# Attention and routed expert MLPs on one Trainium2 core: the overflow loop moved ahead of the last block's output, eight buffers of gathered rows, no weight conversion in a chunk with an output

## The chip, the core and the metric

The kernel runs on one core of one Trainium2 chip. The core has a matrix engine (PE, whose weight loads are listed apart as PEld), a vector engine (DVE), an activation engine (ACT), a general engine (POOL) that here also starts the gathers and scatters of rows, and a queue (SP) that starts the plain transfers. Each engine works through its own list of instructions in the order in which the program wrote them; engines wait for each other by semaphores. The metric is the device time of one execution in microseconds (us). Lower is better.

## The reference

The first half is attention inside chunks of 64 tokens, for 8 batches, 8 heads, 576 tokens and a head width of 64. Its output, seen as 4608 rows of 512 numbers, is `x`. The second half sends each row through one of eight experts, but only if its skip score is positive:

```python
skip_score = x @ w_skip
do_compute = skip_score > 0
out = x.copy()
xc = x[do_compute]
logits = xc @ w_gate
e_idx = np.argmax(logits, axis=1)
probs = softmax(logits)
gate_w = probs[np.arange(len(xc)), e_idx]
for e in range(E):
    mask = e_idx == e
    h = np.maximum(xc[mask] @ w1[e], 0.0)      # 512 -> 1024
    y[mask] = gate_w[mask, None] * (h @ w2[e]) # 1024 -> 512
out[do_compute] = xc + y
```

So the number of rows of each expert is known only while the kernel runs.

## The kernel before

The program has one launch and, in time, two stages.

**Stage 1, attention and routing (about the first 150 us).** 36 tiles of 128 tokens run through a software pipeline (lines 733 to 790): scores, exponent, transposes, products, then the logits and the routing, which gives each row a place in the list of its expert. The rows `x` are written to the output tensor as they come.

**Stage 2, the experts.** The experts are sorted by their number of rows, and each rank has a fixed capacity, cut into blocks of at most 128 rows (`BLOCKS`, line 50): 464, 400, 288, 288, 280, 248, 232 and 112 rows. 22 blocks form nine units: rank 0 is split in two (256 and 208 rows), and each other rank is one. In the text, unit 2 is the one with 400 rows, units 3 and 4 have 288, unit 5 has 280, unit 6 has 248, unit 7 has 232 and unit 8 has 112. Unit 0 and the first products of stage 2 overlap the end of stage 1. Rows beyond the capacities would be done by the overflow loop at the end (`For_i`, line 975), which runs a number of times that is computed on the chip (`nend`) and may be zero. Where it is zero, each engine still has to load the number, branch past the body and pass the loop's closing waits; these instructions carry the lines 974 and 975 in the profile.

To keep float32 accuracy in 16-bit products, every number is held as a high and a low half, and each product is three: high by high, high by low, low by high. One unit runs so:

1. *First layer*, `l1_steps` (line 512). The hidden width of 1024 is cut into `FC` = 8 chunks. For each chunk twelve matmuls are issued: eight with the high half of the chunk's weights, then four with the low half. `l1_out` follows with one ACT instruction (relu, line 527) and one DVE instruction (the low half, line 528). Three PSUM buffers `hp` take turns.
2. *Second layer*, `l2_steps` (line 540): 24 matmuls of 512 columns for a block of 128 rows, in four steps of six.
3. *Output of a block*, `blk_out` (line 555): one DVE instruction per part (line 561) that adds the gathered row, and then a scatter of the rows (POOL, line 221). Blocks of at most 32 rows have four parts, blocks of at most 64 have two. `blk_out` is a generator kept in the list `prev`, and `out_prev` advances it by one part; so a block's output is issued later, between the products of the next block or, for the last block of a unit, between the chunks of the next unit's first layer.

**Weights.** The weights arrive as float32, one chunk of both layers at a time (512 KB, `load_chunk`, line 206, four staging buffers, started by SP), and are turned into high and low halves by `conv_chunk` (line 212): an ACT instruction (line 217) for the high half and a DVE instruction (line 218) for the low half. There are 56 of these in stage 2, ranks 1 to 7 by 8 chunks, and three sets of converted weights.

What sets the place of a conversion in the order is a pacing clock written out by hand (lines 881 to 897). Each chunk and each step of six matmuls adds an amount of nanoseconds to `clock` by calling `spent`; whenever it reaches `PACE` = 2800, 2800 is taken off and one conversion, the next in the fixed order, is issued at that place of ACT's and DVE's lists. Before the matmuls of a chunk are issued, `need` issues at once whatever conversions up to that chunk haven't been issued yet.

```python
for m, done in enumerate(l1):
    if done:
        out_prev()
        spent(5 * n)
```

Here `done` is true once per chunk, and `n` is the number of rows of the unit. In the second layer each step adds 1280, and a step that also prepares the next unit's rows (`blk_xt`: transposes on PE, line 502, then ACT line 503 and DVE line 506) adds 1280 to the clock without issuing a conversion. The program keeps this order: the list is built under a manual schedule.

**Rows.** The rows of a block are fetched by `blk_gather` (line 491, an indirect transfer issued by POOL, line 221) into one of `XGB` = 6 buffers `xg`, which are cleared at the start (line 202). After block b has been issued, gathers up to block b + `XGB` - 1 are (line 966).

Of the kernel before, what the change touches and what calls it, by code (L numbers as in the profile page):

```python
# [32 lines left out]
FIRST = 3  # L33
EARLY = (3, 3, 4)
FIRST_UNIT = 2
XGB = 6
WSETS = 3
PACE = 2800.0
W_AT = (12, 14, 16, 18, 20, 22, 24, 26)
# [64 lines left out]
def moe_attention_kernel(ctx: ExitStack, tc: tile.TileContext, qk: bass.AP, vo: bass.AP, cst: bass.AP, crow: bass.AP, wall: bass.AP, out: bass.AP):  # L104
# [95 lines left out]

    for _ in range(XGB):
        nc.gpsimd.memset(spool.tile([P, DM], F32, name="xg", bufs=XGB), 0.0)

# [16 lines left out]
    def rows_dma(key, **kw):  # L220
        ins = nc.gpsimd.indirect_dma_start(**kw)  # L221
        ins = getattr(ins, "ins", ins)
        tc.declare_no_dep(ins, group=key, reason="row sets of different transfers are disjoint")
        tc.add_to_no_dep_group(key, ins)
# [33 lines left out]
    def bank(k=None):  # L258
        if k is None:
            turn[0] ^= 1  # L260
            k = turn[0]
        return ps_s.tile([P, DM], F32, name=f"sp{k}")
# [228 lines left out]
    def blk_gather(rec, n=P, rows=NTOK):  # L491
        xg = spool.tile([P, DM], F32, name="xg", bufs=XGB)
        rows_dma("out", out=xg[:n], out_offset=None, in_=out[:rows, :], in_offset=bass.IndirectOffsetOnAxis(ap=rec[0][:n], axis=0), bounds_check=rows - 1, oob_is_err=False)
        return xg
# [17 lines left out]
    def l1_steps(xt, w, ht, n, alloc, need):  # L512
        for fc in range(FC):
            need(fc)
            hp = alloc()[:, :n]
            m = 0
            for a, b in ((0, 0), (0, 1), (1, 0)):
                for j in range(KC):
                    nc.tensor.matmul(hp, w()[:, a, fc, j * P:(j + 1) * P], xt[:, b, j, :n], start=(m == 0), stop=(m == 11))  # L519
                    m += 1  # L520
                if not a:
                    yield 0
            l1_out(ht, hp, fc, n)
            yield 1
# [5 lines left out]
    def take(it, n):  # L530
        while n and next(it, it) is not it:
            n -= 1

    def l2_tiles(n):
        return 4 if n <= P // 4 else 2 if n <= P // 2 else 1

    def l2_parts(n):
        return ((0, P // 2), (P // 2, n - P // 2)) if P // 2 < n <= 3 * P // 4 else ((0, n),)
# [16 lines left out]
    def blk_out(yy, rec, xg, n=P):  # L555
        ys = spool.tile([P, DM], F32, name="x")
        for y, (lo, m) in zip(yy, l2_parts(n)):
            r = slice(lo, lo + m)
            cg = l2_tiles(m)
            for c in range(cg):  # L560
                nc.vector.scalar_tensor_tensor(ys[r], y[c * P // cg:c * P // cg + m], rec[1][r], ys[r] if c else xg[r], op0=ALU.mult, op1=ALU.add)  # L561
                if lo + m < n or c < cg - 1:
                    yield
        rows_dma("out", out=out, out_offset=bass.IndirectOffsetOnAxis(ap=rec[0][:n], axis=0), in_=ys[:n], in_offset=None, bounds_check=NTOK - 1, oob_is_err=False)
# [84 lines left out]
    BIGQ = 1 << 30  # L649
# [141 lines left out]
    n = NT + 3  # L791
# [79 lines left out]
    def feed_load():  # L871
        while queue and len(pend) < (STB if len(EARLY) in xgs else 1):
            p, fc = queue[0]
            if p >= WSETS and last[p - WSETS] >= unit[0] or not sec:
                return
            queue.pop(0)
            if p not in sec_e:
                sec_e[p] = nc.sync.value_load(sec["sexp"][0:1, p:p + 1], min_val=0, max_val=NE - 1)
            pend.append((p, fc, load_chunk(sec_e[p], fc)))

    clock = [0.0]

    def feed_conv():
        feed_load()
        if pend:
            conv_chunk(*pend.pop(0))
            feed_load()

    def spent(ns):
        clock[0] += ns  # L890
        if clock[0] >= PACE:
            clock[0] -= PACE
            feed_conv()

    def need(p, fc):
        while any(k == p and f <= fc for k, f, *_ in queue + pend):
            feed_conv()

    prev = []

    def ahead(m):
        if m < NB_ and m not in recs_b:
            p, b, _ = blocks[m]
            if "rec" in sec:
                q = p * QB + b
                recs_b[m] = tuple(r[:, q:q + 1] for r in sec["rec"])
# [7 lines left out]
    def fetch_next():  # L914
        m = next((m for m in range(min(upto[0] + 1, NB_)) if m not in xgs), NB_)
        ahead(m)
        fetch(m)
        return m in xgs

    def out_prev(n=1):  # L920
        while prev and n:
            if next(prev[0], prev) is prev:
                prev.pop(0)
            n -= 1

    xt, ht = xt0, ht0
    for i, (p, bs, offs, n) in enumerate(units):
        unit[0] = i
        if i:
            l1 = l1_steps(xt, lambda: wsets[p], ht, n, lambda: ps_h.tile([P, DM], F32, name="hp"), lambda fc: need(p, fc))  # L930
        if i == 0:
            feed_load()
            l1 = ()
        for m, done in enumerate(l1):
            if done:
                out_prev()
                spent(5 * n)
            if m % 4 == 1:
                fetch_next()
        w, hc = wsets[p], ht  # L940
        nxt = units[i + 1] if i + 1 < NU else None
        todo = []
        if nxt:
            xt = bpool.tile([P, 2, KC, NMAX], F16, name="xt", bufs=2)
            ht = bpool.tile([P, 2, FC, NMAX], F16, name="ht", bufs=2)
            todo = list(zip(nxt[1], nxt[2]))
        total = sum(FC // l2_tiles(m) // 2 for b in bs for _, m in l2_parts(blocks[b][2]))
        at = 0
        for k, (b, o) in enumerate(zip(bs, offs)):
            for m in range(b + 1, b + 8):  # L950
                ahead(m)
            nb = blocks[b][2]
            y = [bank() for _ in l2_parts(nb)]
            for _ in l2_steps(y, hc, w, o, nb):
                at += 1
                take(steps, 1)
                out_prev()
                if todo and at >= total - 1 - (TLEAD if i else LLEAD) * len(todo):
                    m, o2 = todo.pop(0)
                    fetch(m)  # L960
                    blk_xt(xt[:, :, :, o2:o2 + blocks[m][2]], xgs[m], blocks[m][2])
                    clock[0] += 1280
                elif i:
                    spent(1280)
            prev.append(blk_out(y, recs_b[b], xgs[b], nb))
            upto[0] = b + XGB - 1
            while fetch_next() and i:
                pass
        for m, o2 in todo:
            blk_xt(xt[:, :, :, o2:o2 + blocks[m][2]], xgs[m], blocks[m][2])  # L970
    take(steps, BIGQ)
    out_prev(BIGQ)

    lend = nc.values_load(sec["nend"][0:1, 0:1], min_val=0, max_val=NJ)  # L974
    with tc.For_i(0, lend, 1) as si:
        ex = nc.sync.value_load(sec["oexp"][0:1, bass.ds(si, 1)], min_val=0, max_val=NE - 1)
        key = "over"
        for fc in range(FC):
            conv_chunk(key, fc, load_chunk(ex, fc))
        base = spool.tile([1, 1], F32, name="base")  # L980
        nc.vector.tensor_copy(base, sec["orow"][0:1, bass.ds(si, 1)])
        rb = ps_t.tile([P, DM], F32, name="rk")[:, :1]
        nc.tensor.matmul(rb, onesf, base, start=True, stop=True)
        at = spool.tile([P, NT], F32, name="at")
        nc.vector.tensor_tensor(at, aiall, rb.to_broadcast([P, NT]), op=ALU.subtract)
        cp = ps_t.tile([P, DM], F32, name="rk")[:, :NV]
        for t in range(NT):
            am = spool.tile([P, P], F16, name="am", bufs=1)
            nc.vector.tensor_tensor(am, C("iota"), at[:, t:t + 1].to_broadcast([P, P]), op=ALU.is_equal)
            nc.tensor.matmul(cp, am, recs[:, :, t], start=(t == 0), stop=(t == NT - 1))  # L990
        rv = spool.tile([P, NV, 1], F32, name="rv")
        nc.vector.tensor_copy(rv[:, :, 0], cp)
        rec = finish_rec(rv, "over")
        xg = blk_gather(rec)
        xt = bpool.tile([P, 2, KC, NMAX], F16, name="xt", bufs=2)[:, :, :, :P]
        ht = bpool.tile([P, 2, FC, NMAX], F16, name="ht", bufs=2)
        blk_xt(xt, xg)
        y = [bank()]
        take(l1_steps(xt, lambda: wsets[key], ht, P, lambda: ps_h.tile([P, DM], F32, name="hp"), lambda fc: None), BIGQ)
        take(l2_steps(y, ht, wsets[key], 0, P), FC)  # L1000
        take(blk_out(y, rec, xg), BIGQ)
    man.__exit__(None, None, None)


# [37 lines left out]
```

## Time and profile before

| | us |
|---|---|
| three runs | 345.41, 350.34, 353.88 |
| median | 350.34 |
| the profiled execution | 348.78 |
| its span, first to last instruction | 347.0 |
| mean granted clock of the matrix engine, share of full | 0.985 |

The time of an execution is 1.78 us more than the span of its instructions. The table below gives the busy time of each engine in a few parts of the span, by the profile's view of windows, in us.

| part | length | PE | DVE | ACT | POOL |
|---|---|---|---|---|---|
| 0 to 40 | 40 | 34.56 | 18.51 | 26.08 | 15.31 |
| 80 to 120 | 40 | 37.23 | 31.84 | 29.94 | 20.77 |
| 160 to 200 | 40 | 40.00 | 33.38 | 20.37 | 13.29 |
| 200 to 240 | 40 | 39.42 | 27.91 | 19.14 | 12.31 |
| 280 to 300 | 20 | 19.49 | 15.36 | 9.15 | 7.26 |
| 320 to 330 | 10 | 10.00 | 4.29 | 2.54 | 1.58 |
| 340 to 347 | 7 | 0.00 | 0.00 | 0.00 | 0.00 |

A row of the profile's list of groups reads: line, engine, operation, result and operands by the program's names, shapes, number; then the busy time of all of them in us, the mean of one in ns, and the idle time of the engine just before them with what ended it. A row of the timeline starts with the start and the length in us, and a bracket at its end is the idle time of that engine before it, with the instruction that ended it. The list of one line's instructions gives the shortest, the median and the longest of them in ns, and the first and last start in us; an engine's name with a q is its sequencer (loads of registers, branches, semaphores).

### The profile page before, as it was taken

The numbers are of one execution on the slowest core, as the hardware profiler recorded it, in microseconds if no ns is written. First come the engines' busy times: TensorE is split into PE (matmuls) and PEld (weight loads), VectorE is DVE, ScalarE is ACT, GpSimd is POOL, SyncE is SP. The second block draws the span as 40 slices with busy tenths as digits, with TensorE's granted clock in tenths as the row PEclk, the third lists the DMA queues.
The fourth block names the chain that finished last, engine by engine and source line by source line (L and its number), as shares of the span: only waits on it lengthen the run. The fifth ranks groups of instructions, "written<-read, shape, count | busy, mean of one in ns | idle before, by whom it ended". The sixth has DMA issues, their size and how long they took to land. (4 is left out here: it accounts for less than half of the span.)

```text
span 347.0 us, 10921 instructions
## 1 busy us (share of the span) xinstructions
PE 322.8 (93%) x4388; PEld 221.0 (64%) x4388; DVE 242.4 (70%) x539; ACT 195.1 (56%) x345; POOL 131.2 (38%) x158
## 2 busy tenths in 40 slices
PE   7889898998997999999999999999999999999980
PEld 3567676776675777659555446647647658587750
DVE  1645676987796887987889857876777779667420
ACT  3777787987784895516546344545444445455210
POOL 4423354463637456845050532242343353020111
PEclk9999999999998999999999999999999999999996
DMA  7999999998997992039375877668658767574000
GB/s 237 394 388 362 378 324 321 329 359 291 311 318 256 301 368 95 2 107 383 109 266 170 288 250 238 189 191 270 193 179 278 226 205 228 183 230 133 33 26 29
DMA packets 34408, 81.86 MB, mean 236 GB/s; under 512 B 4255, under 2 KB 4256, under 8 KB 34354
## 3 DMA queue, kind: packets, MB, share of 16 engines
q1 hardware_dynamic: 31250, 71.79, 62.1%
q0 software_dynamic: 3104, 9.33, 7.6%
q8 instruction: 36, 0.59, 0.7%
q14 instruction: 18, 0.15, 0.2%
HBM read 67.07 MB, written 14.17 MB: 234 GB/s over the span
## 5 line engine op out<-in xcount | busy, mean ns | idle before, releaser
L551 PE MATMUL sp<-wset,ht 128*128 128x512 f16 (+7 forms) x552 | 102.8, 379 | 0.0
L519 PE MATMUL hp<-xt,wset 128*128 128x288 f16 (+6 forms) x768 | 85.9, 273 | 0.9 <-DVE ht L528 0.9
L519 PEld LDWEIGHTS <-wset 128*128 128x128 f16 x768 | 69.3, 98 | 18.3 <-issue 3.4
L551 PEld LDWEIGHTS <-ht 128*128 128x128 f16 (+7 forms) x552 | 45.6, 101 | 45.1 <-issue 2.1
L218 DVE SCALAR_TENSOR_TENSOR wset<-wst,wset 128x1024 f16<-128x1024 f32 x56 | 67.6, 1217 | 9.2 <-ACT wset L217 9.1
L221 POOL DMA_INDIRECT out<-x,recsi x18 | 24.3, 1351 | 101.1 <-DVE x L561 87.7
L217 ACT ACTIVATE wset<-wst 128x1024 f16<-128x1024 f32 x56 | 57.8, 1048 | 1.8 <-DMA wst<-in_wall 1.8
L253 POOL TENSOR_TENSOR px<-sc,mx 128x512 f32<-128x512 f32 x36 | 38.0, 1058 | 53.4 <-DVE mx L251 30.6
L527 ACT ACTIVATE ht<-hp 128x288 f16<-128x288 f32 (+6 forms) x64 | 24.5, 383 | 56.0 <-PE hp L519 54.8
L528 DVE SCALAR_TENSOR_TENSOR ht<-hp,ht 128x288 f16<-128x288 f32 (+6 forms) x64 | 26.1, 422 | 17.9 <-ACT ht L527 17.3
L251 DVE TENSOR_REDUCE mx<-sc 128x8 f32<-128x512 f32 x36 | 24.4, 678 | 19.7 <-ACT sc L246 19.1
L503 ACT ACTIVATE xt<-xt 128x512 f16<-128x512 f32 (+7 forms) x20 | 10.3, 513 | 43.3 <-PE xt L502 43.3
L289 PE MATMUL xq<-sv,pz 64*64 64x65 f32 x1152 | 27.4, 226 | 6.5 <-issue 5.8
L289 PEld LDWEIGHTS xq<-sv,pz 64*64 64x64 f32 x1152 | 21.6, 135 | 13.6 <-issue 10.6
L241 PE MATMUL sc<-st 64*64 64x64 f32 x1152 | 25.9, 227 | 3.2 <-DMA st<-in_qk 1.8
L322 ACT ACTIVATE xc<-sp 128x512 f32<-128x512 f32 x36 | 21.4, 595 | 11.4 <-PE sp L316 10.1
L241 PEld LDWEIGHTS sc<-st 64*64 64x64 f32 x1152 | 20.9, 136 | 10.7 <-issue 4.6
L246 ACT ACTIVATE sc<-sc 128x512 f32<-128x512 f32 x36 | 21.5, 597 | 9.9 <-PE sc L241 8.6
L298 DVE TENSOR_TENSOR xa<-xq,rr 128x512 f32<-128x512 f32 x36 | 24.9, 692 | 1.2
L221 POOL DMA_INDIRECT xg<-out,recsi x18 | 23.2, 1287 | 5.5 <-issue 3.7
L273 PE MATMUL sp<-csb,px 128*128 128x128 f32 x144 | 23.9, 289 | 0.4 <-ACT sc L246 0.4
L506 DVE SCALAR_TENSOR_TENSOR xt<-xt 128x512 f16<-128x512 f32 (+7 forms) x20 | 11.7, 585 | 17.2 <-ACT xt L503 16.7
(157 smaller groups left out, 374.0 us busy)
## 6 DMA issues: line engine op xcount, KB each, us to landing
wst<-in_wall SPq DMA_DIRECT2D x56, 512.0 KB, 4.2
st<-in_qk SPq DMA_DIRECT2D x72, 256.0 KB, 5.0
sv<-in_vo SPq DMA_DIRECT2D x36, 260.0 KB, 5.1
out<-xa SPq DMA_DIRECT2D x36, 256.0 KB, 5.2
wst<-in_wall SPq DMA_DIRECT2D x16, 256.0 KB, 5.2
csb<-in_cst SPq DMA_DIRECT2D x1, 312.5 KB, 5.0
xg<-out,recsi POOLq DMA_INDIRECT x18, 5.6
out<-x,recsi POOLq DMA_INDIRECT x18, 4.8
```

The lines of the kernel that those rows point to most:

```text
L217: nc.scalar.activation(w[:, 0, fc, :], st, AF.Copy, scale=SW)
L218: nc.vector.scalar_tensor_tensor(w[:, 1, fc, :], st, SW, w[:, 0, fc, :], op0=ALU.mult, op1=ALU.subtract)
L221: ins = nc.gpsimd.indirect_dma_start(**kw)
L241: nc.tensor.matmul(sp[halves[c], a, j], st[halves[r], 0, w], st[halves[r], 1, w], start=(j == 0), stop=True, skip_group_check=True)
L251: nc.vector.tensor_reduce(mx, T[t]["sc"], axis=AX.X, op=ALU.max)
L253: nc.gpsimd.tensor_tensor(px, T[t].pop("sc"), mx.unsqueeze(2).to_broadcast([P, H, CH]), op=ALU.subtract)
L289: nc.tensor.matmul(xq[w, a, j * (D + 1):(j + 1) * (D + 1)], pz[r, j, w], v[r, c, j], start=(j == 0), stop=True, skip_group_check=True)
L298: nc.vector.tensor_tensor(x.rearrange("p (j a d) -> p a j d", a=2, d=D), xq[:, :, :, :D], rr.to_broadcast([P, 2, KC, D]), op=ALU.mult)
L519: nc.tensor.matmul(hp, w()[:, a, fc, j * P:(j + 1) * P], xt[:, b, j, :n], start=(m == 0), stop=(m == 11))
L527: nc.scalar.activation(ht[:, 0, fc, :n], hp, AF.Relu)
L528: nc.vector.scalar_tensor_tensor(ht[:, 1, fc, :n], hp, 0.0, ht[:, 0, fc, :n], op0=ALU.max, op1=ALU.subtract)
L551: nc.tensor.matmul(y[c * P // cg:c * P // cg + n], ht[:, a, fc, o:o + n], w[:, b, fc, P * KC:], start=(f == 0 and m == 0), stop=(f == fw - ...
```

## The change

Three things are changed. The number of `xg` buffers, and with it the reach of the gathers, goes from six to eight. In the first layer, a chunk in which a part of an output is issued adds 2.5 n instead of 5 n to the pacing clock, and it doesn't call `spent`, so no conversion is issued in it; a chunk without an output is as before. And ahead of the overflow loop, outputs are issued only until one block is left; the last block's output is issued behind the loop.

```diff
-XGB = 6
+XGB = 8
...
         for m, done in enumerate(l1):
-            if done:
+            if done and prev:
                 out_prev()
+                clock[0] += 2.5 * n
+            elif done:
                 spent(5 * n)
             if m % 4 == 1:
                 fetch_next()
...
     take(steps, BIGQ)
-    out_prev(BIGQ)
+    while len(prev) > 1:
+        out_prev()
 
     lend = nc.values_load(sec["nend"][0:1, 0:1], min_val=0, max_val=NJ)
     with tc.For_i(0, lend, 1) as si:
...
         take(blk_out(y, rec, xg), BIGQ)
+    out_prev(BIGQ)
     man.__exit__(None, None, None)
```

## The prediction

> **What bounds the kernel now.** I read the page's first part, then the windows of stage 2, then the waits of the matrix engine.
>
> ```profile
> span 347.0 us, 10921 instructions
> PE 322.8 (93%) x4388; PEld 221.0 (64%) x4388; DVE 242.4 (70%) x539; ACT 195.1 (56%) x345; POOL 131.2 (38%) x158
> ```
>
> ```profile
> 160.00:200.00 40.00, 40.00 (x273) 23.30 (x271) 33.38 (x50) 20.37 (x31) 13.29 (x9) 1.00 0.66 228
> 200.00:240.00 40.00, 39.42 (x286) 24.01 (x285) 27.91 (x38) 19.14 (x30) 12.31 (x11) 1.00 0.72 227
> 320.00:330.00 10.00, 10.00 (x96) 7.05 (x95) 4.29 (x9) 2.54 (x6) 1.58 (x2) 1.00 0.08 29
> ```
>
> ```profile
> PE hp L519 <- DVE ht L528: 0.9, 2, 0.5
> PE xt L502 <- DMA xg<-out,recsi: 0.6, 1, 0.6
> ```
>
> In the windows the first number behind the length is PE's busy time: 40.00 of 40, 39.42 of 40, 10.00 of 10, at full clock (1.00). From 155 us to the last product the matrix engine sets the time, and every us in which it stands still is a us of the end. The waits say how little is left to win there: 0.9 us in which the first layer waited for a PSUM buffer that DVE had not emptied, and 0.6 us for one late gather. So the question is whether the change makes PE wait, and what it does behind PE's last product.
>
> **Part 1: conversions move later, and some arrive when PE needs them.** All 56 conversions stay; only their places move. I walked the clock through the nine units by the code, once by the old rule and once by the new. The walk by the old rule ends with the last conversion in the second layer of unit 7, ahead of unit 8, and the trace has it there: the last L218 starts at 324.91 and unit 8 begins at 327.07.
>
> ```profile
> 327.07 4.88 PE L519 MATMUL hp<-xt,wset 128*128 128x112 f16 x96
> 323.83 1.05 ACT L217 ACTIVATE wset<-wst 128x1024 f16<-128x1024 f32 x1
> 324.91 1.23 DVE L218 SCALAR_TENSOR_TENSOR wset<-wst,wset 128x1024 f16<-128x1024 f32 x1 [0.32 <-ACT wset L217]
> ```
>
> By the new rule, with chunks counted from 0:
> - Unit 1 starts at 2560 by either rule; it adds 520 + 7 x 1040 in its chunks and 7 x 1280 in its steps, less six conversions at 2800, so unit 2 (400 rows) starts at 2520 (old rule: 3040) with chunks 0 to 5 of its own expert converted. The block before it has 80 rows, six parts, so its chunks 0 to 5 all carry an output and convert nothing; the clock goes to 2520 + 6 x 1000 = 8520. Chunk 6 isn't converted: `need` issues it right ahead of its matmuls, and chunk 7 comes from the clock, right behind chunk 6. By the old rule both were issued by chunk 1.
> - Units 3, 4 and 5 start at 1160, 1720 and 2280 (old: 2080, 2720, 560) and follow blocks with four parts. The backlog is caught up in time: unit 5's chunk 7 is issued after its chunk 4, two chunks ahead.
> - Unit 6, from 2600 (old: 880): chunks 6 and 7 are issued after its chunks 4 and 5, one chunk ahead each.
> - Unit 7, from 680 (old: 1440): chunk 6 is issued after chunk 4, chunk 7 by `need`, right ahead.
> - Unit 8 (112 rows) starts at 20 (old: 1360) with chunks 0 to 4 converted. Its eight chunks add only 280 + 7 x 560, so `need` issues 5, the clock 6, `need` 7, each right ahead of its matmuls.
>
> What one such place costs, from these groups:
>
> ```profile
> L218 DVE SCALAR_TENSOR_TENSOR wset<-wst,wset 128x1024 f16<-128x1024 f32 x56 | 67.6, 1217 | 9.2 <-ACT wset L217 9.1
> L217 ACT ACTIVATE wset<-wst 128x1024 f16<-128x1024 f32 x56 | 57.8, 1048 | 1.8 <-DMA wst<-in_wall 1.8
> L519 PE MATMUL hp<-xt,wset 128*128 128x400 f16 x96 | 16.4, 333 | 0.0
> L519 PE MATMUL hp<-xt,wset 128*128 128x248 f16 x96 | 10.5, 269 | 0.5 <-DVE ht L528 0.5
> L519 PE MATMUL hp<-xt,wset 128*128 128x232 f16 x96 | 9.7, 263 | 0.0
> L519 PE MATMUL hp<-xt,wset 128*128 128x112 f16 x96 | 4.9, 213 | 0.0
> ```
>
> ```profile
> 187.29 0.50 ACT L527 ACTIVATE ht<-hp 128x400 f16<-128x400 f32 x1 [0.58 <-PE hp L519]
> 187.69 1.05 ACT L217 ACTIVATE wset<-wst 128x1024 f16<-128x1024 f32 x1
> 314.15 0.36 ACT L527 ACTIVATE ht<-hp 128x232 f16<-128x232 f32 x1 [0.82 <-PE hp L519]
> 314.41 1.05 ACT L217 ACTIVATE wset<-wst 128x1024 f16<-128x1024 f32 x1
> 316.33 6.64 PE L551 MATMUL sp<-wset,ht 128*128 128x512 f16 x30
> 316.53 0.36 ACT L527 ACTIVATE ht<-hp 128x232 f16<-128x232 f32 x1 [0.82 <-PE hp L519]
> ```
>
> The conversion stands on ACT behind the relu of the chunk before, and that relu starts 0.20 us after PE could go on (316.33 and 316.53). The conversion starts 0.40 us after the relu for 400 rows and 0.26 for 232 (the pairs above); for 248 I take 0.28, for 112 rows 0.16, the same steps down. Then 1.05 for the high half, 0.05 to hand over: PE stands for 0.20 + 0.40 + 1.05 + 0.05 = 1.70 us in unit 2, 1.46 in unit 8. The low half starts when the high half ends (324.88 and 324.91) and takes 1.22. PE needs it after eight of the twelve matmuls: 8 x 16.4/96 = 1.37 us in unit 2, so it is nearly there; 0.41 us in unit 8, so PE waits 0.82 more. A chunk lasts 2.05, 1.31, 1.21 and 0.61 us (a group's busy time by 8).
>
> - Unit 2: 2 x 1.70, and 0.1 as DVE issues the output's last part ahead of the low half: 3.5.
> - Unit 6: chunk 6's high half is ready 1.58 after chunk 4, chunk 5 ends after 1.31: 0.3, its low half 0.4; chunk 7's low half 0.4 behind the one before: 1.1.
> - Unit 7: chunk 6 0.35 + 0.42, chunk 7 1.56 + 0.40: 2.7.
> - Unit 8: 3 x (1.46 + 0.82): 6.9.
>
> Sum 14.2. Nothing hides it: PE has nothing else in its list. Behind the late conversions stand the following relus on ACT and low halves on DVE, which wait with PE. The nearest bounds: if only the high halves counted, 3.4 + 0.3 + 1.9 + 4.4 = 10.0; for the upper end I add 0.1 us of handover to each of the fifteen waits, 15.7. The second layers take up to four conversions in a block (unit 2's first): 4 x 1.22 = 4.9 us of DVE under 24 matmuls, 24/30 of 6.64 = 5.3 us, so these stay hidden. Staging buffers and SP's loads follow the conversions, three chunks ahead, and cost nothing.
>
> **The clock after long stalls.** The granted clock in three windows:
>
> ```profile
> 50.10:53.50 3.40, 2.08 (x67) 1.00 0.87 299
> 104.61:108.02 3.41, 1.42 (x37) 1.00 0.97 352
> 108.02:111.43 3.41, 3.41 (x60) 0.50 0.75 234
> ```
>
> PE was busy 1.42 of 3.41 us, and the next 3.41 us ran at 0.50; with 2.08 of 3.40 the clock stayed. In unit 8's stalls PE works 0.61 us of every 2.89, 21%, for some 8.7 us, longer than two such windows. So I expect half clock at the end of unit 8 and into the last block's products, until a well-filled window has passed: between half a window and one and a half, mean about 3.4 us at half clock, 1.7 lost, and 0.3 in unit 8's low products: 2.0. Bounds: 0 to 4. In unit 2 PE works 2.05 of 3.75 us, 55%, on the side that stayed.
>
> The Trainium skill's page "TensorE: Matmul & The Clock Gate", section "Why this matters for your kernels", sets the line elsewhere: no idle gap over about 3 us between bursts. No stall here reaches that (2.3 us), so by that rule the clock stays. But the gap before 107.16 was 1.99 us long, and this trace throttled after it.
>
> **Part 2: what the lighter chunks save.** No conversion between the outputs of small blocks: the 0.9 us that PE waited for DVE goes; bounds 0 (if the conversions, now bunched in the chunks behind the outputs, load DVE as much) and 0.9. I take 0.9, since the outputs' parts and the conversions no longer meet in one chunk and three buffers lie between PE and DVE.
>
> **Part 3: eight buffers.** Block 10's gather is issued two blocks earlier, 0.6 us saved, bounds 0 and 0.6. Two more clearings on POOL at the start:
>
> ```profile
> 0.72 2.83 POOL L202 MEMSET xg<- 128x512 f32 x6 [0.29 <-POOLq L1035]
> 7.83 1.04 POOL L253 TENSOR_TENSOR px<-sc,mx 128x512 f32<-128x512 f32 x1 [4.28 <-DVE mx L251]
> ```
>
> About 1 us, under the 4.28 us in which POOL waits; without that cover, 1 us. The number of gathers and the traffic are the same, and no gather in POOL's list gets a new wait: its buffer is free at the same place.
>
> **Part 4: the end.**
>
> ```profile
> 337.18 0.75 DVE L561 SCALAR_TENSOR_TENSOR x<-sp,sel,xg 112x512 f32<-112x512 f32 x1 [4.61 <-PE sp L551]
> 338.21 0.96 POOL L221 DMA_INDIRECT out<-x,recsi  x1 [7.78 <-DVEq L975]
> DMA to landing us min/median/max: 3.2/3.2/3.2
> ```
>
> ```profile
> L975 POOLq EVENT_SEMAPHORE  x13: 17/43/1256, 338.7 to 342.2; - x13
> L975 PEldq COMPARE_BRANCH  x3: 97/192/3393, 333.8 to 342.6; - x3
> L975 POOLq INC_SWDGE_SEM  x1: 1069/1069/1069, 338.8 to 338.8; - x1
> L1038 POOLq DRAIN  x3: 46/98/3668, 342.5 to 346.7; - x3
> L1038 POOLq EVENT_SEMAPHORE  x4: 17/17/17, 346.2 to 346.9; - x4
> L1035 POOLq DRAIN  x1: 188/188/188, 0.3 to 0.3; - x1
> ```
>
> Now: last product ended just ahead of the output at 337.18, scatter 338.21, landed 341.4 (3.2 later); then twelve closing waits of the loop on each engine until 342.3, POOL's drain of 3.67 until 346.1, and 0.8 of final handshakes. With the change the loop's load, branch, POOL's 1.07 us and most of the closing waits run under the last products. But the output on DVE and the scatter on POOL stand behind those waits, which include PE's last product: some 0.3 us later (a few waits of 0.05). The scatter lands at 341.7; the list of waits, 0.9 us, is over by then. The drain is the unknown: if it runs while the scatter is under way, the end comes 3.1 us earlier, if it follows the landing, 0.6. No row tells which (188 ns at the program's start, 3668 here); I take the middle, 1.8.
>
> **The sum.** 347.0 + 14.2 + 2.0 - 0.9 - 0.6 - 1.8 = 359.9 us of span; with the 1.78 around it (348.78 against 347.0), 361.7. The profiled execution lies 1.6 under the median of the three runs, 350.34, so a median may come out as much higher. Against the median the change is +3.2%.
>
> **Rivals.**
> - *The clock stays* (the rule above, and a threshold below 21%): 359.7. For it: the throttled window was one of small products, unlike these. Chance 0.20.
> - *Only the high halves count*, as DVE is otherwise idle and PE's list is deep: 10.0 of stalls, no throttle: 347.0 + 10.0 - 3.3 + 1.78 = 355.5, +1.5%. Against: 1.22 us is three times the 0.41 of unit 8's eight matmuls. Chance 0.15.
> - *The clock also falls in unit 7*, whose stalls come to half of a window: 1.7 more twice, as the next window may be as thin: 365.1. Chance 0.08.
> - *The loop's end becomes the path.* PE's branch past the loop takes 3.39 us; if DVE's output must wait for it, the end is 3.4 later instead of 1.8 earlier: 366.9. Against: in the trace the other engines passed their last waits without a stop of that kind, PE's semaphore stands ahead of that branch. Chance 0.08.
> - *Not slower*: the conversions are issued earlier than the code's order, ACT taking one before the relu that waits for PE, so that all stalls are hidden: 347.0 - 3.3 + 1.78 = 345.5. It decides if under 3.3 of the 16.2 us remain. Against: DVE's order in the trace is the code's, conversion by conversion. Chance 0.05.
>
> **How the numbers follow.** The likeliest, with 0.44, gives 361.7. The range from 354.5 to 367.0 takes in the high-half rival with an early drain and, above, the throttled ones. Two per cent of 350.34 is about what a measurement can tell, 357.3. Above it lie the likeliest, the clock's two rivals and the loop's, 0.80, less some for sizes: slower 0.74, same 0.22, faster 0.04.
>
> **What would show it.** Right: nine late conversions, two each in units 2, 6 and 7 and three in unit 8, with gaps of PE that L217 or L218 ends; unit 8's first layer lasting 11 to 13 us instead of 4.9; granted clock 0.50 near the end; the drain of 3.67 us begun before the last scatter has landed; the waits for DVE's ht and for the late gather gone. Wrong: conversions in the trace ahead of the chunks named, or PE without gaps there.

## The result, and the profile after

| | before | changed |
|---|---|---|
| median of the runs, us | 349.60 (4 runs, 345.41 to 353.88) | 362.41 (4 runs, 360.27 to 364.64) |
| the profiled execution, us | 348.78 | 364.64 |
| its span, us | 347.0 | 362.5 |
| granted clock, share of full | 0.985 | 0.976 |

The changed kernel is slower: 1.044 of the time before, 95% interval 1.038 to 1.050. Medians are over all runs, and the ratios here and below compare fast runs alone (a run over 1.5% above the fastest of its kernel counts as slow). The page of the changed kernel begins:

```profile
span 362.5 us, 10917 instructions
PE 328.0 (90%) x4388; PEld 222.4 (61%) x4388; DVE 243.5 (67%) x539; ACT 195.1 (54%) x345; POOL 129.3 (36%) x160
```

ACT's busy time is the one of before to the tenth, PE has the same 4388 instructions with 5.2 us more of busy time, and the span is 15.5 us longer. So hardly any work was added; what grew are waits and, by a smaller part, the time of PE's products. The waits of the matrix engine in stage 2, where before stood 0.9 us for DVE's `ht` and 0.6 us for a gather:

```profile
PE hp L519 <- ACT wset L217: 9.1, 7, 1.9
PE hp L519 <- DVE wset L218: 2.4, 7, 0.7
```

Both old waits are gone, and PE now waits for converted weights, seven times for a high half and seven times for a low one. The groups of the first layer, by shape (busy time, mean, then idle time ahead of them):

```profile
L519 PE MATMUL hp<-xt,wset 128*128 128x288 f16 x192 | 23.9, 286 | 0.0
L519 PE MATMUL hp<-xt,wset 128*128 128x400 f16 x96 | 16.9, 333 | 3.3 <-ACT wset L217 3.1 <-DVE wset L218 0.2
L519 PE MATMUL hp<-xt,wset 128*128 128x280 f16 x96 | 11.6, 283 | 0.0
L519 PE MATMUL hp<-xt,wset 128*128 128x248 f16 x96 | 10.9, 269 | 0.4 <-DVE wset L218 0.2
L519 PE MATMUL hp<-xt,wset 128*128 128x232 f16 x96 | 10.4, 263 | 2.2 <-ACT wset L217 1.6 <-DVE wset L218 0.6
L519 PE MATMUL hp<-xt,wset 128*128 128x112 f16 x96 | 7.0, 234 | 5.8 <-ACT wset L217 4.5 <-DVE wset L218 1.4
```

The waits stand in units 2, 6, 7 and 8. Units 3, 4 and 5 (288 and 280 rows) have none. Unit 8's busy time is also higher, 7.0 us for the 4.9 of before, and its mean 234 ns for 213: its products ran slower. The timeline of one late chunk of unit 8 (start, length, engine; in brackets the idle time before and what ended it):

```profile
342.11 0.26 ACT L527 ACTIVATE ht<-hp 128x112 f16<-128x112 f32 x1 [1.74 <-PE hp L519]
342.27 1.05 ACT L217 ACTIVATE wset<-wst 128x1024 f16<-128x1024 f32 x1
342.41 0.27 DVE L528 SCALAR_TENSOR_TENSOR ht<-hp,ht 128x112 f16<-128x112 f32 x1 [0.78 <-ACT ht L527]
343.35 1.22 DVE L218 SCALAR_TENSOR_TENSOR wset<-wst,wset 128x1024 f16<-128x1024 f32 x1 [0.67 <-ACT wset L217]
343.38 0.93 PE L519 MATMUL hp<-xt,wset 128*128 128x112 f16 x8 [1.30 <-ACT wset L217]
344.63 0.55 PE L519 MATMUL hp<-xt,wset 128*128 128x112 f16 x4 [0.33 <-DVE wset L218]
345.22 0.26 ACT L527 ACTIVATE ht<-hp 128x112 f16<-128x112 f32 x1 [1.91 <-PE hp L519]
```

It is read from top to bottom as one chain: relu of the chunk before, high half, eight products, low half, four products, and the next relu. From relu to relu this chunk takes 345.22 - 342.11 = 3.11 us, with its products at half clock; before, a chunk of this unit took 0.61.

The windows over the end of unit 8 and the last block, each 3.41 us long, as the half clock in these profiles lasts 3.41 us or two or three times that (length, PE busy, ..., granted clock in the third number from the end):

```profile
338.49:341.90 3.41, 0.87 (x14) 0.62 (x12) 1.60 (x3) 1.21 (x2) 0.32 (x1) 1.00 0.23 64
341.90:345.31 3.41, 1.65 (x16) 1.01 (x12) 1.50 (x2) 1.29 (x3) 0.00 (x0) 0.50 0.00 0
345.31:348.73 3.42, 1.91 (x14) 1.46 (x15) 1.59 (x3) 1.39 (x3) 0.00 (x0) 0.50 0.00 0
348.73:352.14 3.41, 3.41 (x10) 1.74 (x9) 0.18 (x1) 0.00 (x0) 0.00 (x0) 0.50 0.01 2
352.14:355.55 3.41, 3.30 (x16) 1.71 (x14) 0.00 (x0) 0.00 (x0) 0.00 (x0) 1.00 0.00 0
```

One window in which PE worked 0.87 of 3.41 us, and then three at half clock; the last of the three is full of products, and only the one after it is granted full clock. The 24 products of the last block take 7.34 us (348.10 to 355.44) for 5.34 before.

And the end: the last output and its scatter, then the rows of the loop's line and of the final handshakes.

```profile
L561 DVE SCALAR_TENSOR_TENSOR x<-sp,sel,xg x1: 751/751/751, 355.8 to 355.8; 112x512 f32<-112x512 f32 x1
L221 POOL DMA_INDIRECT out<-x,recsi x1: 960/960/960, 356.9 to 356.9; - x1
```

```profile
L978 PEldq COMPARE_BRANCH  x3: 101/193/3253, 351.4 to 360.3; - x3
L978 POOLq INC_SWDGE_SEM  x1: 1050/1050/1050, 338.3 to 338.3; - x1
```

```profile
L1042 POOLq EVENT_SEMAPHORE  x4: 17/17/17, 361.7 to 362.4; - x4
L1042 POOLq DRAIN  x3: 46/104/5002, 356.6 to 362.2; - x3
```

The output starts 0.4 us behind the last product (355.44), POOL's 1.05 us for the loop lie at 338.3, far ahead, and PE's branch of 3.25 us runs beside the scatter. The span ends 7.05 us behind the last product, where it was 9.83.

Unit by unit, from the timelines of the two profiles, the stretch from unit 1's first product to the end of the span grew from 191.7 to 204.6 us:

| term | before, us | changed, us | difference |
|---|---|---|---|
| first layer of unit 2 | 16.41 | 20.19 | +3.78 |
| of unit 4 | 12.47 | 11.93 | -0.54 |
| of unit 6 | 11.00 | 11.25 | +0.25 |
| of unit 7 | 9.68 | 12.57 | +2.89 |
| of unit 8 | 4.88 | 12.85 | +7.97 |
| second layer of unit 2 (late gather) | 19.00 | 18.38 | -0.62 |
| the last block's products | 5.34 | 7.34 | +2.00 |
| behind the last product | 9.83 | 7.05 | -2.78 |
| sum | | | +12.95 |

The other 2.6 us of the 15.5 lie in stage 1, which the change touches only through the two more buffers (two clearings, and gathers issued earlier): unit 1 began at 157.9 us for 155.3. The profiles of the experiments below show this start anywhere between 150.1 and 159.0.

### The profile page after: what moved, and what is told of

Same layout as the page of the kernel before. It is cut to its first block, busy times and chain, and to the rows that moved or that the text cites. A ratio compares the mean times of both kernels' runs of the same rounds, so it can differ in the third digit from the quotient of the medians.

```text
span 362.5 us, 10917 instructions
## 1 busy us (share of the span) xinstructions
PE 328.0 (90%) x4388; PEld 222.4 (61%) x4388; DVE 243.5 (67%) x539; ACT 195.1 (54%) x345; POOL 129.3 (36%) x160
## 5 line engine op out<-in xcount | busy, mean ns | idle before, releaser
L551 PE MATMUL sp<-wset,ht 128*128 128x512 f16 (+7 forms) x552 | 104.8, 384 | 0.0
L519 PE MATMUL hp<-xt,wset 128*128 128x288 f16 (+6 forms) x768 | 89.4, 276 | 11.7 <-ACT wset L217 9.1
L218 DVE SCALAR_TENSOR_TENSOR wset<-wst,wset 128x1024 f16<-128x1024 f32 x56 | 67.5, 1221 | 15.5 <-ACT wset L217 14.9
L551 PEld LDWEIGHTS <-ht 128*128 128x128 f16 (+7 forms) x552 | 46.5, 103 | 46.2 <-issue 4.0
L221 POOL DMA_INDIRECT out<-x,recsi x18 | 20.6, 1147 | 123.6 <-DVE x L561 118.0
L241 PE MATMUL sc<-st 64*64 64x64 f32 x1152 | 27.2, 227 | 7.4 <-DMA st<-in_qk 4.5
L221 POOL DMA_INDIRECT xg<-out,recsi x18 | 25.2, 1402 | 5.5 <-issue 3.1
L278 ACT ACTIVATE pz<-sp 128x512 f32<-128x512 f32 x36 | 21.5, 598 | 2.8 <-PE sp L273 1.9
```

The source lines that it names most:

```text
L218: nc.vector.scalar_tensor_tensor(w[:, 1, fc, :], st, SW, w[:, 0, fc, :], op0=ALU.mult, op1=ALU.subtract)
L241: nc.tensor.matmul(sp[halves[c], a, j], st[halves[r], 0, w], st[halves[r], 1, w], start=(j == 0), stop=True, skip_group_check=True)
L551: nc.tensor.matmul(y[c * P // cg:c * P // cg + n], ht[:, a, fc, o:o + n], w[:, b, fc, P * KC:], start=(f == 0 and m == 0), stop=(f == fw - ...
```

## The experiments

In each edit the base is named. Ratios are to the kernel before on the same chip, with the 95% interval.

**Each part of the change alone.** The kernel before with only the new rule for the first layer's chunks:

```diff
-            if done:
+            if done and prev:
                 out_prev()
+                clock[0] += 2.5 * n
+            elif done:
                 spent(5 * n)
```

> The kernel before with only the new rule for chunks with an output (no conversion, 2.5 n on the clock); six buffers, output ahead of the loop. Theory (late conversions are the whole loss): slower by 14 to 18 us, a ratio near 1.045 to 1.05, with the first layer of unit 8 near 12.8 us instead of 4.9, that of unit 2 near 20.2 instead of 16.4, the 0.9 us of waits for DVE's ht gone, and the late gather of 0.6 us still there. Rival (the loop's new place or the two more buffers bring a good part of the loss): slower by clearly less than 14 us.

Measured: 363.62 us, ratio 1.047 (1.039 to 1.054). In its profile unit 2's first layer takes 20.19 us, unit 7's 12.57 and unit 8's 12.82, as in the changed kernel, and PE's waits for weights are nearly the same:

```profile
PE hp L519 <- ACT wset L217: 9.1, 7, 1.9
PE hp L519 <- DVE wset L218: 2.7, 7, 0.7
PE xt L502 <- DVE wset L218: 1.0, 1, 1.0
```

The third row stands where the kernel before had its late gather, at the transposes of the block of 32 rows for unit 3. They read no converted weights (`xt<-csb,xg`), so the engine that the row names can't be what they needed; the gather is the likely cause, but its landing is not on record. From unit 1 to the end this run takes 207.5 us, for 204.6 in the changed kernel and 191.7 before. So this part alone makes the whole loss, and more than the whole: the other parts give some back. The half clock came too, for two windows instead of three (340.89 to 347.71), so its last block took 6.68 us instead of 7.34.

Only the loop moved, in the kernel before:

```diff
     take(steps, BIGQ)
-    out_prev(BIGQ)
+    while len(prev) > 1:
+        out_prev()
...
         take(blk_out(y, rec, xg), BIGQ)
+    out_prev(BIGQ)
```

> The kernel before with only the loop moved ahead of the last block's output. Theory (POOL's drain runs while the last scatter is under way): faster by 2 to 3 us, ratio 0.992 to 0.994, the span behind PE's last product 7.0 us instead of 9.9. Rival (the drain follows the scatter's landing): faster by 0.6 us at most. Second rival (the output waits for PE's branch of 3.4 us): slower by 3 us. Nothing changes ahead of the last product but run-to-run shifts.

Measured: 345.60 us, ratio 0.9945 (0.9905 to 0.9984), and 7.07 us behind the last product for 9.83. The drain's row is this:

```profile
L1040 POOLq DRAIN  x3: 46/104/5022, 336.3 to 341.9; - x3
```

It began at 336.35, ahead of the scatter's issue (336.58 to 337.54), and ended at 341.37; the scatter had landed at 339.52. Of the three theories the first holds. In this run PE didn't wait for a gather, though it had six buffers.

Only eight buffers, in the kernel before:

```diff
-XGB = 6
+XGB = 8
```

> The kernel before with only eight xg buffers. Theory: the late gather of 0.6 us goes and nothing else changes: 0 to 0.6 us faster, ratio 0.998 to 1.000. Rival (the 2.6 us by which the first stage of the changed kernel ran later in its profile come from the buffers: two more clearings on POOL, earlier gathers): 2 to 3 us slower, ratio 1.006 or more.

Measured: 348.70 us, ratio 1.0035 (1.0000 to 1.0070). It isn't faster. PE's waits hold the 1.0 us for DVE's `ht` and none for a gather. Whether two more buffers cost anything stays open: the interval reaches from nothing to 2.4 us. That they set the later start of stage 2 isn't borne out by the profiles: in this run's own profile, the second longest of its twelve runs (352.12 us), unit 1 began latest of all, at 159.0 us, but with eight buffers it also began at 150.1, 150.8, 151.7, 154.3, 156.3, 157.9 and 158.2 us in the profiles of the seven other runs, and with six at 153.6, 153.8 and 155.3.

Loop and buffers, that is the changed kernel with the old rule for the clock:

```diff
-            if done and prev:
+            if done:
                 out_prev()
-                clock[0] += 2.5 * n
-            elif done:
                 spent(5 * n)
```

> The changed kernel with the old rule for the clock in the first layer: both other parts kept. Theory: the conversions are all in time again, so the two gains show: 2.5 to 3.5 us faster than before, ratio 0.990 to 0.993; the waits of 0.9 us for DVE's ht stay. Rival (buffers or loop take part in the loss): not faster than before.

Measured: 343.87 us, ratio 0.9885 (0.9809 to 0.9961). The conversions are in time, the stretch from unit 1 to the end is 188.6 us against 191.7 before, and the waits for `ht` stay at 1.0 us. With this run and the first the cause is placed on both sides: the rule alone brings the loss, and without it the loss is gone.

**What in the rule does it.** For these the changed kernel was run again as a neighbour on the same chip:

> The changed kernel once more, as the neighbour of the next three on the same chip. Both theories: slower than before by 12 to 16 us; half clock for two or three windows of 3.41 us from the late conversions of unit 8 on, and the last block's 24 products in about 6.5 to 7.4 us instead of 5.3.

Measured: 363.10 us, ratio 1.046 (1.039 to 1.053); half clock from 342.87 for three windows, the last block's products in 7.71 us.

The rule has two halves: no conversion in the chunk, and half the credit on the clock. The changed kernel with the full credit:

```diff
-                clock[0] += 2.5 * n
+                clock[0] += 5 * n
```

> The changed kernel with 5 n instead of 2.5 n on the clock for a chunk with an output; still no conversion there. Theory (units 6, 7 and 8 run short because the clock gets too little, unit 2 because six chunks in a row convert nothing): only chunks 6 and 7 of unit 2 are late, the first layer of unit 2 takes about 20.2 us, units 6, 7 and 8 take 11.0, 9.7 and 4.9 to 5.1 us, no half clock; 347.0 + 3.8 - 0.9 - 2.8: even with the kernel before within 1 us. Rival (the missing conversions in the output chunks are the loss by themselves): most of the 13 us remain.

Measured: 348.41 us, ratio 1.002 (0.997 to 1.006). What is left is unit 2:

```profile
L519 PE MATMUL hp<-xt,wset 128*128 128x400 f16 x96 | 16.9, 333 | 3.3 <-ACT wset L217 3.1 <-DVE wset L218 0.2
L519 PE MATMUL hp<-xt,wset 128*128 128x248 f16 x96 | 10.3, 269 | 0.0
L519 PE MATMUL hp<-xt,wset 128*128 128x232 f16 x96 | 9.7, 263 | 0.0
```

Unit 8's first layer is back at 5.01 us and the clock stays. Units 6 and 7 are at 10.33 and 9.68 us. So the missing credit is most of the loss: without it the clock issues fewer conversions than there are, and the debt falls due at the end, where a chunk is shortest. The six chunks in a row without a conversion cost unit 2's 3.8 us.

**The half clock.** The changed kernel with products whose results are never read, in the waits of unit 8:

```diff
+            if done and p == NE - 1 and 14 <= m < 23:
+                idle = ps_t.tile([P, DM], F32, name="rk")
+                for _ in range(24):
+                    nc.tensor.matmul(idle[:, :P], ones, ones, start=True, stop=True)
             if done and prev:
                 out_prev()
```

> The changed kernel with 24 products of 128 columns, whose results nobody reads, behind chunks 4, 5 and 6 of unit 8, so that PE works while it waits for the late conversions. Theory (half clock comes from PE's thin work in these waits): the clock stays at 1.00 through unit 8, the last block's products take 5.3 us, and the time is 2 to 3 us lower than that of the changed kernel, though PE does more. Rival (the half clock has another cause, such as the power drawn over the whole stage): the clock falls as before and the time is the same or higher.

Measured: 358.93 us, ratio 1.036 (1.030 to 1.043), 4.2 us under its neighbour's median. PE's timeline from the fifth chunk's end, with the added products as L938:

```profile
332.19 1.50 PE L938 MATMUL rk<-ones 128*128 128x128 f16 x24
334.19 0.57 PE L519 MATMUL hp<-xt,wset 128*128 128x112 f16 x8 [0.50 <-ACT wset L217]
335.44 0.37 PE L519 MATMUL hp<-xt,wset 128*128 128x112 f16 x4 [0.69 <-DVE wset L218]
335.65 1.50 PE L938 MATMUL rk<-ones 128*128 128x128 f16 x24
...
341.52 5.34 PE L551 MATMUL sp<-wset,ht 128*112 128x512 f16 x24
```

```profile
334.20:341.50 7.30, 5.22 (x84) 4.48 (x85) 4.19 (x5) 2.42 (x4) 0.00 (x0) 1.00 0.02 6
341.50:346.90 5.40, 5.36 (x28) 3.01 (x25) 0.28 (x1) 0.26 (x1) 0.00 (x0) 1.00 0.01 2
```

PE works 5.22 of 7.30 us, where the window that brought the half clock on had 0.87 of 3.41, the clock stays at 1.00, and the last block takes 5.34 us. The waits for weights themselves stay: unit 8's first layer is 12.44 us. So thin work brought the half clock on, and its price was 2.0 us in the last block (2.4 against the neighbour's 7.71) and 12.85 - 12.44 = 0.4 in unit 8; the rest of the 4.2 lies within what stage 1 moves from profile to profile.

**A version that keeps what helps.** Full credit, and the old rule in units 1 and 2:

```diff
-            if done and prev:
+            if done and prev and i > 2:
                 out_prev()
-                clock[0] += 2.5 * n
+                clock[0] += 5 * n
             elif done:
+                out_prev()
                 spent(5 * n)
```

> The changed kernel with 5 n on the clock, and with the old rule in units 1 and 2: no conversion in a chunk with an output from unit 3 on, and none late. Theory: no wait of PE in any first layer, neither for weights nor for DVE's ht (0.9 us), and the loop's gain of 2.8: 3.5 to 4.5 us faster than before, ratio 0.987 to 0.990, the best of all versions. Rival (the waits for ht only move): the same as the kernel with the loop and the buffers alone, 2.8 us faster.

Measured: 345.06 us, ratio 0.9946 (0.9902 to 0.9990). Its first layers have no wait left, here the three shapes that had one:

```profile
L519 PE MATMUL hp<-xt,wset 128*128 128x400 f16 x96 | 16.4, 333 | 0.0
L519 PE MATMUL hp<-xt,wset 128*128 128x248 f16 x96 | 10.3, 269 | 0.0
L519 PE MATMUL hp<-xt,wset 128*128 128x112 f16 x96 | 5.0, 213 | 0.0
```

From unit 1 to the end it takes 187.2 us, the shortest of all: 4.5 under the kernel before and 1.4 under loop and buffers alone. In time it is clearly faster than the changed kernel, and faster than the kernel before by little: the interval ends just under 1, and less was gained than the expected ratio of 0.987 to 0.990. Against the loop alone or loop and buffers, the times can't tell it apart: their intervals overlap, and in the profiles the start of stage 2 shifts by several us.

**From where the drain counts.** The version above with four clearings of an unused buffer behind the last scatter:

```diff
     out_prev(BIGQ)
+    for _ in range(4):
+        nc.gpsimd.memset(spool.tile([P, DM], F32, name="late", bufs=1), 0.0)
```

> The kernel with the old rule in units 1 and 2 and full credit, and behind the last block's scatter four clearings on POOL of about 0.5 us each, of a buffer nobody uses. It asks from where POOL's drain counts, in the span behind PE's last product (7.07 us without them). Theory (the drain takes 3.67 us from the end of POOL's last instruction, whatever that is): the span's end comes about 2 us later, 9.0 to 9.2 us behind the last product. Rival (it counts from the scatter, whose issue or landing it waits for): the clearings run inside the 3.67 us and the end stays at 7.1 us.

Its one run took 345.71 us. The end of its profile:

```profile
335.76 0.96 POOL L221 DMA_INDIRECT out<-x,recsi  x1 [8.14 <-DVE x L561]
336.71 2.30 POOL L1008 MEMSET late<- 128x512 f32 x4
```

```profile
L1045 POOLq EVENT_SEMAPHORE  x4: 17/17/17, 342.8 to 343.5; - x4
L1045 POOLq DRAIN  x3: 46/104/4233, 338.5 to 343.3; - x3
```

The span ends 9.21 us behind the last product, 2.1 later. The drain ended at 342.70, 3.69 us behind the last clearing (339.01). With the scatter as POOL's last instruction the drain ended 3.8 us behind it (341.37 and 337.54 with the loop moved alone). So it counts from POOL's last instruction, a scatter or a clearing, and not from the scatter's landing, which came at 338.71 here.

## Why the prediction was right

The forecast of 361.7 met a median of 362.41, and by its own steps:

- *The places.* The walk of the clock named nine late conversions in units 2, 6, 7 and 8 and none in 3, 4 and 5. The waits stand in exactly these units. Of the fifteen waits in the sum the rows count fourteen; the shortest are not counted there, such as that of unit 6's chunk 6, which began at 297.99, just behind the end of its high half at 297.94.
- *The price of a late conversion*, 14.2 us in all. At full clock the runs give 3.78 in unit 2 (forecast 3.5), 0.92 in unit 6 (1.1; 11.25 against 10.33 in the version without waits), 2.89 in unit 7 (2.7) and 7.56 in unit 8 (6.9; 12.44 with the added products against 4.88): 15.2. In unit 8 the late chunks themselves cost what was worked out: at full clock, in the run with the added products, 2.93 us from chunk 5's first product to chunk 6's and from there to chunk 7's, less 0.61, is 2.3. What came on top stands ahead of the first of them: the relu behind chunk 4 began 0.80 us behind the start of that chunk's last product (339.16 and 338.36 in the changed kernel), for 0.25 in the chunk before. What held it is not shown. The low halves wait as forecast: the rival in which only high halves count falls.
- *The clock*, 2.0 forecast, 2.0 in the last block and 0.4 in unit 8 measured. The rival in which the clock stays falls with the windows and with the added products. The Trainium skill's page "TensorE: Matmul & The Clock Gate" (section "Why this matters for your kernels") looks for idle gaps of more than about 3 us; no wait here was longer than 1.9 us by PE's row, and the clock fell. The rival in which it falls in unit 7 too was closer than its 0.08 says. In the changed kernel PE was busy half of one window there and the clock stayed; with the loop moved alone, a window of stage 1 with as much work was followed by half clock. So unit 7 lay where the runs show both outcomes, and that its clock stayed is partly luck:

```profile
321.42:324.83 3.41, 1.72 (x16) 1.20 (x14) 1.62 (x2) 1.31 (x2) 0.00 (x0) 1.00 0.55 163
324.83:328.24 3.41, 3.41 (x18) 1.53 (x16) 2.39 (x3) 3.20 (x4) 0.00 (x0) 1.00 0.46 154
```

```profile
12.17:15.58 3.41, 1.71 (x67) 1.23 (x65) 2.44 (x5) 1.74 (x4) 1.54 (x2) 1.00 1.05 391
15.58:19.00 3.42, 2.24 (x33) 1.65 (x37) 0.00 (x0) 1.05 (x2) 0.54 (x1) 0.50 1.04 385
```

- *DVE's waits for `ht`*, 0.9 forecast: unit 4 gained 0.54 and unit 6 0.67 (11.00 against 10.33), 1.2.
- *The gather*, 0.6: it went in the changed kernel's profile (-0.62). With six buffers such a wait stands in the profile before (0.6) and, most likely, in that of the new rule alone (1.0), but not in that of the loop moved alone; with eight it stands in none of eight profiles. So eight buffers seem to end it, but it is no steady loss, and the times of eight buffers alone don't show a gain.
- *The end*, 1.8 forecast as a middle between 0.6 and 3.1: 2.78. This was the term most off. The drain runs beside the scatter, and the upper bound was nearly right.

The sum of the terms is 12.9 measured and 12.9 forecast, so their errors cancelled: waits and clock were 1.4 larger, gains 1.3 larger. And the forecast for the profiled execution lies 2.9 us under that execution, 364.64, because stage 1 ran 2.6 us later in it and 0.36 more lies around the span (2.14 for 1.78); that the median of 362.41 lies nearer is luck: the four runs reach from 360.27 to 364.64, and the start of stage 2 alone moves by more than that between profiles. *Not slower*, by conversions ahead of their place in the code, and *the loop's end becomes the path* fall as well.

## What to carry to other kernels

A pacing rule that issues work "a little later" must be walked to the end of the program: what it doesn't issue isn't saved but falls due where work is forced, and the price of a forced item is the whole chain from one engine to the next, here some 1.9 us in a long chunk and 2.3 in a short one against nothing when it is early. When conversions are kept out of crowded chunks, keep the credit and check the longest run of such chunks. And work that each engine must pass at the end, a skipped loop for instance, is better put ahead of the last output, where other engines still have work.

## What the runs showed that I had not expected

- POOL's drain at the end was over 3.7 to 3.8 us behind the end of POOL's last instruction: the loop's closing waits and branch in the kernel before (where its row is 3.67 us long), the scatter with the loop moved (3.8), four clearings behind it (3.69). At the program's start it took 0.19. So the span ends about 4.6 us behind POOL's last instruction (357.83 and 362.5 in the changed kernel, 339.01 and 343.6 with the clearings).
- Two waits of PE, of 1.85 and 0.69 us, with 0.87 us of work in a window of 3.41, brought half clock on, and the window that is already full of products still ran at half: three windows, 10.24 us, for some 9.6 us of late chunks (338.5 to 348.1).
- Unit 1 begins anywhere from 150.1 to 159.0 us in the profiles, more than all the gains here together. Small changes to stage 2 are read from the stretch behind that start, which repeats to a few tenths (188.6 us in both kernels with the loop moved and the old rule).
